# A transformer block on one core: three of four LN2 tiles and the attention probabilities transposed by VectorE and DMA instead of TensorE

## The chip, the core and the metric

The kernel runs on one NeuronCore of a Trainium2 chip. Five engines work side by side, each through its own instruction queue in order: TensorE (PE, matrix multiply; its weight loads are shown as PEld), VectorE (DVE), ScalarE (ACT), GpSimd (POOL) and SyncE (SP, which issues DMAs). They wait for each other by semaphores. The metric is the device time of one execution in microseconds (us), lower is better; the page and the traces time a profiled execution.

## What is computed

A diffusion-transformer block over 2 batches of 256 tokens, model width D = 1152, 2 heads of 576, feed-forward width F = 4608, all in bf16:

```
mod = (silu(c) @ w_mod).reshape(B, 6, 1, D)
shift_a, scale_a, gate_a, shift_m, scale_m, gate_m = [mod[:, i] for i in range(6)]
h = layernorm(x) * (1 + scale_a) + shift_a
q, k, v = (h @ wqkv) split by head
attn = softmax(q @ k.T * Dh ** -0.5)
x = x + gate_a * ((attn @ v) @ wo)
h2 = layernorm(x) * (1 + scale_m) + shift_m
return x + gate_m * (gelu(h2 @ w_fc1) @ w_fc2)
```

## The kernel before

The 512 tokens are four tiles of 128 (tiles 0 and 1 are batch 0, tiles 2 and 3 batch 1), the width D is KT = 9 chunks of 128, F is JT = 36 chunks. A matrix product needs its contracted dimension on the 128 partitions, so what LayerNorm and softmax leave with tokens on partitions has to be transposed before the next product.

The program records every operation with a cost (`S.op`, `S.unit`), finds the dependencies from the memory that operations read and write, and a list scheduler (`schedule`, line 281) fixes each engine's order. PE and SP keep the order in which the code records them. ACT, DVE and POOL are ordered by the planner: the ready operation with the longest remaining path goes first, by the planned costs. Waits on semaphores follow from the dependencies; two readers of one PSUM bank on different engines are ordered too. PSUM has 8 banks.

The steps around the change, in PE's order:

- q, k (the last 9 q and k chunks), then scores S for the four (batch, head) pairs, numbered `idx = 2*batch + head`, in the order idx 0, 2, 1, 3.
- `s_and_softmax` (line 993): DVE row maximum `smax` and `snb`; ACT `sexp` (two activations with row sums); DVE reciprocal `sri`; DVE `spn` multiplies the 128x512 probabilities by it (L1013).
- `pt_transposes` (line 1017): four PE transposes of 128x128 per idx into PSUM and one copy to SBUF, `PT_ev` (DVE or ACT). They stand between the products of `v_proj` (12 of 9 matmuls, 384 columns each, evacuated by ACT).
- `rows` (72 matmuls, shift and scale of the MLP), three more `v_proj`, then `pv_halves` and `pv`, which take the transposed probabilities `PTS` as moving operand.
- The attention gate: `attn_gate` (line 1056) sums 18 DVE operations `ga_b_kt` of 1.4 us, reduces them, and stores the gate row to DRAM from POOL's queue (`st_ga0`, `st_ga1`); SP loads it back broadcast to 128 partitions (`ld_g0`, `ld_g1`).
- `wo_tile(t)` (line 1153): three products of 384 columns; for each DVE `wo_t1` (L1165, times the gate, which frees the PSUM bank) and POOL `wo_x1` (L1166, plus x); then DVE `bn`, `aggr`, `veps`, POOL `rstd` (L744), DVE `nmr2` (L1170) and ACT `xn2` (L1171), which writes the normalized tile `XN2[t]`.
- `xn2_T(t)` (line 1175): nine PE transposes of that tile into two PSUM banks; nine operations `h2T` apply scale and shift on the way to `H2T`, on DVE (L1187) or ACT (L1190).
- `fc1_tile(f, tok0, ntok)` (line 1193): nine matmuls with `H2T` as moving operand, then ACT Gelu (L1200). The first F0 = 9 of 36 chunks are done for batch 0 alone (256 tokens), later for batch 1; the others for 512 tokens at once. `xn2_T(0)` stands before `wo_tile(3)`, `xn2_T(1)` before its last third, `xn2_T(2)` after four and `xn2_T(3)` after seven of the batch-0 fc1 chunks.
- `mlp_gate`: 18 long DVE operations after the last `h2T`; then fc2, 13 products of 36 matmuls.

SP's queue holds the weight loads in the recorded order; `ld_wo` follows the K projection, the fc1 quarters 0 and 1 follow `rows`, then the two gate loads, quarters 2 and 3, the MLP gate weights `ld_gm` and two parts of w_fc2.

Of the kernel before, what the change touches and what calls it, by code (L numbers as in the profile page):

```python
# [9 lines left out]
SEM_LAT = 120.0  # L10
# [161 lines left out]
class Sched:  # L172
    def __init__(self):
# [8 lines left out]
        self.first = {}  # L182

# [9 lines left out]
    def instr(self, fn, reads=(), writes=(), name="", unit=None, is_out=False):  # L193
# [10 lines left out]
        return ins  # L204

# [75 lines left out]
    def schedule(self, dma_bw=385.0, dma_issue=650.0, dma_lat0=900.0, dma_lat1=600.0, verbose=False):  # L281
# [44 lines left out]
        while scheduled < n:  # L326
# [39 lines left out]
            for f, uid in fin_now:  # L366
                for s in units[uid].succ:
                    ndeps[s.uid] -= 1
                    at = max(avail_time.get(s.uid, 0.0), f + (SEM_LAT if True else 0.0))
# [139 lines left out]
F0 = 9  # L509
# [34 lines left out]
def build_kernel(nc, x, c, wqkv, wo, w_mod, w_fc1, w_fc2, out):  # L544
# [5 lines left out]
    with (  # L550
# [62 lines left out]
        H2T = HK  # L613
        OT = sb(O_HX, 9216).rearrange("p (k t) -> p k t", k=KT)
        PP = [sb(O_P + i * 1024, 1024).rearrange("p (j k) -> p j k", j=2) for i in range(4)]
        PTS = [sb(O_PT + i * 1024, 1024).rearrange("p (j k) -> p j k", j=2) for i in range(4)]
# [351 lines left out]
        dma(WO, wo_v, D * D * 2, "ld_wo", run=2304)  # L968

# [23 lines left out]
        def s_and_softmax(b, h):  # L993
# [18 lines left out]
            rib = ri.unsqueeze(2).broadcast_to([P, 2, 256])  # L1012
            u = dve(c_dve_tt16(512), lambda e: e.tensor_tensor(out=pp, in0=pp, in1=rib, op=ALU.mult), [pp, ri], [pp], "spn_%d" % idx)  # L1013
            if idx % 2 == 1:
                S.order_after(ga_units[(1, 7) if idx == 1 else (0, 8)], u)

        def pt_transposes(b, h):
            idx = b * 2 + h
            bank = s_bank[(b, h)]
            S.unit("pe", 4 * c_mm(128), "PT_%d_%d" % (b, h))  # L1020
            for kjt in range(2):
                for jq in range(2):
                    tr(ps16(bank, kjt * 256 + jq * 128, 128), PP[idx][:, jq, kjt * 128:(kjt + 1) * 128], IDENT)
            copy_on("dve" if b == 0 else "act", PTS[idx].rearrange("p j k -> p (j k)"), ps16(bank, 0, 512), 512, True, "PT_ev%d" % idx)

        v_banks = [0, 1, 2]
        v_rr = [0]

        def v_proj(t, ci):
            bank = v_banks[v_rr[0] % 3]  # L1030
# [25 lines left out]
        def attn_gate():  # L1056
# [25 lines left out]
            last_red[0] = dve(200, lambda e: e.transpose(GTA, GBA), [GBA], [GTA], "ga_t")  # L1082
            lin = scratch[0].rearrange("b (g c) -> (b g) c", c=32)
            dma(lin[0:64].rearrange("(j p) c -> p j c", j=2), GTA[:, 0:64].rearrange("p (j c) -> p j c", j=2), 4096, "st_ga0", eng="pool")
            dma(lin[64:72], GTA[0:8, 64:96], 512, "st_ga1", eng="pool")
# [32 lines left out]
        PVB = [(6, 7, 0, 1), (3, 4, 0, 1)]  # L1118
# [229 lines left out]
```

## Time and profile before

| What | Value |
|---|---|
| Device time, 3 runs | 242.79 to 243.5 us, median 243.26 us |
| Span of the profiled execution, first to last instruction | 242.5 us |
| Median less that span | 0.76 us |
| Granted TensorE clock, mean | 0.993 |
| Scores to the end of `rows` and V, on PE | about 49 to 75.9 us |
| `pv` and `wo_tile`, on PE | 75.9 to 98.5 us |
| fc1, on PE | 98.5 to about 170 us; fc2 after it |
| HBM read | 50.15 MB, most of it before 155 us |

In the page, busy is the time in which an engine worked; each digit of the slices is a tenth of 6.06 us; idle time is put down to whoever ended it. In the timeline each row has start and duration in us, engine, source line, operation, tiles and count; a bracket gives the idle time before it. Starts of successive operations on one engine are closer than their durations, because neighbours overlap: a step below is the distance between starts.

### The profile page before, as it was taken

To read this page: it belongs to the slowest core of one execution; us is meant where nothing else is said; L and a number is where in the kernel's file an instruction comes from. 1 tells how busy PE (TensorE), PEld (TensorE's weight loads), DVE (VectorE), ACT (ScalarE), POOL (GpSimd) and SP (SyncE) were. 2 spreads that over 40 slices of the span, in tenths; PEclk is the share of its full clock that TensorE was granted. 3 is DMA by queue.
4 is the path that set the end of the run, shared out by engine and by line. 5 is a ranking of instruction groups with operands and counts; after the bars stand their busy time and mean duration, and the time that the engine had idled before them with its cause. 6 is when DMAs were issued, how large, how long until landed. Compare 5 with 4: busy or idle time off the path is not lost.

```text
span 242.5 us, 3957 instructions
## 1 busy us (share of the span) xinstructions
PE 237.3 (98%) x1699; PEld 145.4 (60%) x1699; DVE 121.5 (50%) x229; ACT 67.8 (28%) x136; POOL 19.9 (8%) x36
## 2 busy tenths in 40 slices
PE   6899999999999999999999999999999999999995
PEld 2688844466666666898544444444666566566564
DVE  2654379988996689669999700000022222111112
ACT  4921440435524206973233322222000000000000
POOL 1300000000002276400000110000000000000000
PEclk9979999999999999999999999999999999999999
DMA  6999999999992999999963499100000000000000
GB/s 221 378 370 392 389 392 390 398 413 402 391 352 79 312 374 391 391 348 398 352 198 83 157 313 374 43 0 3 0 16 19 16 16 16 19 16 16 21 27 20
DMA packets 30363, 51.58 MB, mean 213 GB/s; under 512 B 1547, under 2 KB 15755, under 8 KB 30347
## 3 DMA queue, kind: packets, MB, share of 16 engines
q1 hardware_dynamic: 29888, 50.73, 58.9%
q0 software_dynamic: 288, 0.60, 0.8%
q8 instruction: 13, 0.21, 0.4%
q10 hardware_dynamic: 171, 0.01, 0.0%
q14 instruction: 3, 0.02, 0.0%
HBM read 50.15 MB, written 1.19 MB: 212 GB/s over the span
## 4 chain that ended last, share of the span: by engine, by line
PE 95%; DMA 3%; SPq 1%; DVE 0%; issue 0%
PE psum L692 93%; DMA arena<-in_wqkv_dram 3%; PE psum L695 2%; SPq L673 1%; DVE arena L1290 0%; DVE arena L1291 0%
## 5 line engine op out<-in xcount | busy, mean ns | idle before, releaser
L692 PE MATMUL psum<-arena 128*128 128x384 bf16 (+8 forms) x1610 | 234.0, 314 | 2.4 <-POOL arena L718 1.5
L692 PEld LDWEIGHTS psum<-arena 128*128 128x128 bf16 (+2 forms) x1610 | 139.7, 97 | 92.4 <-issue 3.8
L1290 DVE TENSOR_TENSOR arena<-psum,arena 128x384 f32<-128x384 f32 (+2 forms) x13 | 6.8, 526 | 88.6 <-PE psum L692 88.6
L1200 ACT ACTIVATE arena<-psum 128x512 bf16<-128x512 f32 (+1 forms) x45 | 22.8, 512 | 42.1 <-PE psum L692 42.1
L687 ACT ACTIVATE arena<-psum 128x512 bf16<-128x512 f32 (+6 forms) x34 | 18.2, 560 | 37.9 <-PE psum L692 37.9
L1064 DVE SCALAR_TENSOR_TENSOR arena<-arena 128x1152 f32<-128x1152 bf16 x16 | 21.9, 1408 | 0.0
L1095 DVE SCALAR_TENSOR_TENSOR arena<-arena 128x1152 f32<-128x1152 bf16 x16 | 21.4, 1414 | 0.0
L1166 POOL TENSOR_TENSOR arena<-arena 128x384 f32<-128x384 f32 x12 | 10.9, 912 | 11.7 <-DVE arena L1165 9.5
L740 DVE BATCH_NORM_STATS2 arena<-arena 128x6 f32<-128x384 f32 (+1 forms) x18 | 9.5, 549 | 3.8 <-DMA arena<-in_x_dram 3.8
L673 POOL DMA_DIRECT2D dit_scratch<-arena x4 | 2.4, 609 | 96.6 <-DVE arena L1082 60.3
L689 DVE CAST arena<-psum 128x512 bf16<-128x512 f32 x11 | 7.2, 687 | 5.3 <-PE psum L692 5.3
L1165 DVE TENSOR_TENSOR arena<-psum,arena 128x384 f32<-128x384 f32 x12 | 6.7, 556 | 3.7 <-PE psum L692 3.7
L1171 ACT ACTIVATE arena<-arena 128x1152 bf16<-128x1152 f32 x4 | 5.4, 1344 | 9.8 <-DVE arena L1170 9.8
L695 PE MATMUL psum<-arena 128*128 128x128 bf16 (+1 forms) x89 | 7.4, 225 | 0.4 <-DMA arena<-in_c_dram 0.4
L695 PEld LDWEIGHTS psum<-arena 128*128 128x128 bf16 (+1 forms) x89 | 6.3, 102 | 2.2 <-DMA arena<-in_c_dram 1.1
L1291 DVE TENSOR_TENSOR arena<-arena 128x384 bf16<-128x384 f32 (+2 forms) x13 | 6.9, 527 | 0.5
L1190 ACT ACTIVATE arena<-psum,arena 128x128 bf16<-128x128 bf16 x16 | 6.1, 455 | 3.0 <-PE psum L695 2.2
L1187 DVE TENSOR_SCALAR arena<-psum,arena 128x128 bf16<-128x128 bf16 x20 | 5.5, 336 | 2.9 <-PE psum L695 2.9
L1009 ACT ACTIVATE arena<-psum,arena 128x256 bf16<-128x256 f32 x8 | 3.7, 471 | 0.2 <-DVE arena L1006 0.2
L744 POOL TENSOR_TENSOR arena<-arena 128x1 f32<-128x1 f32 x6 | 3.3, 555 | 4.7 <-DVE arena L743 4.5
L1005 DVE TENSOR_REDUCE arena<-psum 128x2 f32<-128x512 f32 x4 | 2.8, 688 | 0.9 <-PE psum L692 0.7
L962 ACT ACTIVATE arena<-arena 128x256 bf16<-128x256 bf16 x6 | 2.5, 495 | 1.5 <-DVE arena L956 1.5
(60 smaller groups left out, 53.9 us busy)
## 6 DMA issues: line engine op xcount, KB each, us to landing
arena<-in_w_fc_dram SPq DMA_DIRECT2D x9, 1152.0 KB, 8.0
arena<-in_w_fc_dram SPq DMA_DIRECT2D x4, 2592.0 KB, 17.6
arena<-in_wqkv_dram SPq DMA_DIRECT2D x18, 288.0 KB, 9.3
arena<-in_w_mod_dram SPq DMA_DIRECT2D x6, 864.0 KB, 12.3
arena<-in_w_mod_dram SPq DMA_DIRECT2D x3, 1728.0 KB, 20.5
arena<-in_wqkv_dram SPq DMA_DIRECT2D x1, 2592.0 KB, 17.6
arena<-in_wo_dram SPq DMA_DIRECT2D x1, 2592.0 KB, 24.9
arena<-in_w_mod_dram SPq DMA_DIRECT2D x1, 2592.0 KB, 18.5
```

What stands on the lines that cost most here:

```text
L687: act(c_act(n), lambda e: e.activation(out=dst, in_=src, func=ACTF.Copy), [src], [dst], name)
L689: return dve(c_dve_psum16(n) if psum16 else c_dve_psum32(n), lambda e: e.tensor_copy(dst, src), [src], [dst], name)
L692: S.instr(lambda e: e.matmul(o, lhsT=l, rhs=r, start=st, stop=sp, **kw), reads=[l, r], writes=[o])
L695: S.instr(lambda e: e.transpose(o, i_, idn), reads=[i_, idn], writes=[o])
L740: dve(550, lambda e, s=s, o=o: e.bn_stats(out=o, in_=s), [s], [o], "bn_%s_%d" % (tag, ci))
L1064: ga_units[(b, kt)] = dve(150 + FG * 1.1, lambda e, o=o, w=w, s1=s1: e.scalar_tensor_tensor(out=o, in0=w, scalar=s1, in1=o, op0=ALU.mult, ...
L1095: u = dve(1300, lambda e, o=o, w=w, s1=s1: e.scalar_tensor_tensor(out=o, in0=w, scalar=s1, in1=o, op0=ALU.mult, op1=ALU.add), [w, s1, o], ...
L1165: dve(550, lambda e, o=o, ga=ga, x1c=x1c: e.tensor_tensor(out=x1c, in0=o, in1=ga, op=ALU.mult), [o, ga], [x1c], "wo_t1_%d_%d" % (t, ci))
L1166: S.op("pool", 930, lambda e, xs=xs, x1c=x1c: e.tensor_tensor(out=x1c, in0=x1c, in1=xs, op=ALU.add), reads=[x1c, xs], writes=[x1c], name=" ...
L1200: act(c_act(ntok), lambda e: e.activation(out=dst, in_=o, func=ACTF.Gelu_apprx_tanh), [o], [dst], "gelu_%d_%d" % (f, tok0))
L1290: dve(c_dve_psum32(w), lambda e, o=o, gm=gm, t1=t1: e.tensor_tensor(out=t1, in0=o, in1=gm, op=ALU.mult), [o, gm], [t1], "fc2_t1_%d_%d" % ( ...
L1291: dve(c_dve_32(w), lambda e, t1=t1, x1c=x1c, ost=ost: e.tensor_tensor(out=ost, in0=t1, in1=x1c, op=ALU.add), [t1, x1c], [ost], "fc2_out_%d ...
```

## The change

The probabilities of all four idx and the LN2 tiles 0, 2 and 3 are transposed without PE. DVE's transpose turns 32x32 blocks, inside groups of 32 partitions; the source is read with a stride so that four DMAs, one per group of 32 tokens, put each turned group onto all 128 partitions with contiguous runs (256 B for the probabilities, 576 B for LN2). The result lies in groups of 32 tokens, and the fc1 and PV operands are read in that form. `spn` moves from one DVE operation per idx to two ACT operations. Scale and shift of the moved tiles work in place in SBUF. Tile 1 keeps its PE transposes.

```diff
+            for jq in range(2):
+                o, aa = pp[:, jq, :], ri[:, jq:jq + 1]
+                act(c_act(256, 1), lambda e, o=o, aa=aa: e.activation(out=o, in_=o, func=ACTF.Copy, scale=aa), [o, aa], [o], "spn_%d_%d" % (idx, jq))
+            src, flat = pp.rearrange("p j (t x c) -> p c (j t) x", t=2, c=4), PTF[idx]
+            dve(c_dve_32(512), lambda e: e.transpose(flat, src), [src], [flat], "PT_turn%d" % idx)
+            for a in range(4):
+                dma(PPF[idx][:, 128 * a:128 * a + 128], flat[32 * a:32 * a + 32, :], P * 256, "mv_pt%d_%d" % (idx, a), run=256)
...
+        H2T = sb(O_HK, 9216).rearrange("p (g k i) -> p k g i", g=16, k=KT)
...
+        TURNED = {0: H2F[3], 2: XN2[0], 3: XN2[1]}
+        def xn2_turn(t):
+            src, flat = XN2[t].rearrange("p (k x c) -> p c k x", k=KT, c=4), TURNED[t]
+            dve(c_dve_32(D), lambda e: e.transpose(flat, src), [src], [flat], "h2turn_%d" % t)
+        def xn2_move(t):
+            b, b0 = t // 2, 0
+            for a in range(4):
+                dma(H2F[t][:, 288 * a:288 * a + 288], TURNED[t][32 * a:32 * a + 32, :], P * 576, "mv_h2_%d_%d" % (t, a), run=576)
+            for kt in range(KT):
+                dst = H2T[:, kt, 4 * t:4 * t + 4, :]
...
+                if kt % 2 if t == 0 else kt % 3 == 2:
+                    act(330, lambda e, dst=dst, s1=s1, s2=s2: e.activation(out=dst, in_=dst, func=ACTF.Identity, scale=s1, bias=s2),
+                        [dst, s1, s2], [dst], "h2T_%d_%d" % (t, kt))
+                    continue
+                last_h2T[0] = dve(220, lambda e, dst=dst, s1=s1, s2=s2: e.tensor_scalar(out=dst, in0=dst, scalar1=s1, scalar2=s2, op0=ALU.mult, op1=ALU.add),
+                    [dst, s1, s2], [dst], "h2T_%d_%d" % (t, kt))
```

`st_ga0` and `st_ga1` go from POOL's queue to SP's. The recorded order after the scores becomes:

```diff
-        v_proj(0, 2)
-        pt_transposes(0, 0)
...
+        dma(WO, wo_v, D * D * 2, "ld_wo", run=2304)
         wfc1_load(0)
-        wfc1_load(1)
+        gate_store()
         for b in range(2):
             dma(GA[b], scratch[0, b].partition_broadcast(P), P * D * 2, "ld_g%d" % b, run=2304)
+        wfc1_load(1)
+        v_proj(0, 2)
+        for t in range(1, 4):
+            for ci in range(NCH):
+                v_proj(t, ci)
+        rows()
         wfc1_load(2)
         wfc1_load(3)
...
         wo_tile(0)
+        xn2_turn(0)
+        xn2_move(0)
+        dma(WGM, wmod_v[:, :, 5 * D:6 * D], D * D * 2, "ld_gm", run=2304)
         wo_tile(1)
         wo_tile(2)
-        xn2_T(0)
+        xn2_turn(2)
         wo_tile(3, {2: lambda: xn2_T(1)})
-        for f in range(0, 4):
-            fc1_tile(f, 0, 256)
-        xn2_T(2)
...
+        xn2_turn(3)
+        xn2_move(2)
+        xn2_move(3)
+        for tok0 in (0, 128):
+            for f in range(0, 3):
+                fc1_tile(f, tok0, 128)
+        for f in range(3, F0):
             fc1_tile(f, 0, 256)
+        wfc2_load(1)
+        wfc2_load(2)
```

F0 rises from 9 to 14: three fc1 chunks are done for tile 0 and for tile 1 apart (128 columns), eleven for batch 0. On ACT, DVE and POOL the order of the softmax, gate and LN2 operations is written out by hand (`in_order`) instead of left to the planner; in it, DVE does `h2T_0` and `h2T_1` between the LN2 statistics of tiles 2 and 3, and the planner puts three Gelus of 128 tokens ahead of ACT's four `h2T_1`:

```diff
+        S.in_order("dve", ["wo_t1_0_0", "wo_t1_0_1", "bn_ln2_0_0", "wo_t1_0_2", "bn_ln2_0_1", "wo_t1_1_0", "bn_ln2_0_2", "aggr_ln2_0", "veps_ln2_0", "wo_t1_1_1", "nmr2_0",
+                           "bn_ln2_1_0", "wo_t1_1_2", "bn_ln2_1_1", "h2turn_0", "wo_t1_2_0", "bn_ln2_1_2", "aggr_ln2_1", "veps_ln2_1", "wo_t1_2_1", "nmr2_1", "bn_ln2_2_0", "wo_t1_2_2", "bn_ln2_2_1", "wo_t1_3_0", "bn_ln2_2_2", "aggr_ln2_2", "veps_ln2_2", "h2T_0_0", "h2T_0_2", "wo_t1_3_1", "nmr2_2", "h2T_0_4", "h2T_0_6", "h2T_0_8",
+                           "h2T_1_0", "h2T_1_1", "h2T_1_2", "h2T_1_3", "h2T_1_4", "bn_ln2_3_0", "wo_t1_3_2", "bn_ln2_3_1", "h2turn_2", "bn_ln2_3_2", "aggr_ln2_3", "veps_ln2_3", "nmr2_3"])
+        S.in_order("act", ["xn2_0", "xn2_1", "h2T_0_1", "h2T_0_3", "h2T_0_5", "h2T_0_7", "h2T_1_5", "h2T_1_6", "h2T_1_7", "h2T_1_8", "xn2_2"])
```

More of the change, by code (lines that the diff above doesn't have):

```diff
@@ L204, in instr, with in_order @@
         return ins
+    def in_order(self, eng, names):
+        by_name = {u.name: u for u in self.units if u.eng == eng}
+        for a, b in zip(names, names[1:]):
+            if by_name[a] not in by_name[b].deps:
+                by_name[b].deps.add(by_name[a])
+                self.loose.add((by_name[a].uid, by_name[b].uid))
     def order_after(self, u, prev):
@@ L508 @@
 NCH = 3
-F0 = 9
+F0 = 14
 KC = 5
@@ L1011, in s_and_softmax @@
             dve(165, lambda e: e.reciprocal(out=ri, in_=rsum), [rsum], [ri], "sri_%d" % idx)
[L1012 to L1026, printed above, removed]
+            for jq in range(2):
[5 more added lines that the diff above has]
+                dma(PPF[idx][:, 128 * a:128 * a + 128], flat[32 * a:32 * a + 32, :], P * 256, "mv_pt%d_%d" % (idx, a), run=256)
+        v_banks = [7, 0, 1, 2]
         v_rr = [0]
         def v_proj(t, ci):
-            bank = v_banks[v_rr[0] % 3]
+            bank = v_banks[v_rr[0] % 4]
             v_rr[0] += 1
@@ L1137, in pv @@
                 for kjt in range(2):
-                    mm(ps32(bank, half * 256, 256), V[:, 2 * b + kjt, g * 128:(g + 1) * 128], PTS[idx][:, kjt, :], kjt == 0, kjt == 1)
+                    mm(ps32(bank, half * 256, 256), V[:, 2 * b + kjt, g * 128:(g + 1) * 128], PTS[idx][:, kjt], kjt == 0, kjt == 1)
             tok = slice(b * 256, (b + 1) * 256)
@@ L1299, in build_kernel @@
             sems = {e: es.enter_context(nc.semaphore("c_" + e)) for e in ENGINES}
-            dma_sems = [es.enter_context(nc.semaphore("d%d" % i)) for i in range(60)]
+            dma_sems = [es.enter_context(nc.semaphore("d%d" % i)) for i in range(66)]
             S.emit(nc, block, sems, dma_sems)
```

67 lines of the change are left out of this document (32 added, 35 removed).

## The prediction

> **What bounds the kernel now.** I read the slices and the busy line first, then the chain of waits, then the timeline of PE.
>
> ```profile
> span 242.5 us, 3957 instructions
> ...
> PE 237.3 (98%) x1699; PEld 145.4 (60%) x1699; DVE 121.5 (50%) x229; ACT 67.8 (28%) x136; POOL 19.9 (8%) x36
> ...
> PE   6899999999999999999999999999999999999995
> ...
> PE 95%; DMA 3%; SPq 1%; DVE 0%; issue 0%
> ```
>
> PE is full from the third slice on, 95% of the chain is PE's own work, and the work on it is the time. An edit gains what it takes off PE's queue, and loses what PE then has to wait for.
>
> The timeline of PE shows what a group of transposes is worth, by the start of what follows it:
>
> ```profile
> 60.98 0.39 PE L695 MATMUL psum<-arena 128*128 128x128 bf16 x4
> 61.21 3.09 PE L692 MATMUL psum<-arena 128*128 128x384 bf16 x18
> ...
> 93.09 0.67 PE L695 MATMUL psum<-arena 128*128 128x128 bf16 x9
> 93.59 3.09 PE L692 MATMUL psum<-arena 128*128 128x384 bf16 x18
> ```
>
> **What comes off PE, and what goes on.** Four groups of probabilities at 61.21 - 60.98 = 0.23 are 0.9 us; three LN2 tiles at 93.59 - 93.09 = 0.50 are 1.5 us; together 2.4. Against it, Gelus of 256 tokens follow each other by 0.983 us (111.47, 112.46, 113.44) and those of 512 by 1.943, so each of the five chunks that are now split costs 2 x 0.983 - 1.943 = 0.023, 0.12 in all. The six products of 128 columns have 54 matmuls; at the transposes' 0.50/9 = 55.6 ns (they too load 128x128 weights each) they take 3.0 us in place of three times 0.983: 0.05. Credit: 2.4 - 0.17 = 2.23 us.
>
> The Trainium skill speaks against those 54: "TensorE: Matmul & The Clock Gate", section "Back-to-back issue gap", gives about 81 ns for 128 columns in a stream where each matmul has its weight load. By it they would cost 54 x 25 = 1.4 us more; the trace's 55.6 ns disagrees.
>
> The operand in groups of 32 tokens: `rows` already streams 288 columns in groups of 32 with gaps. Its 72 matmuls, four side by side, fill the time between the V evacuations at 69.17 and 73.04 less one V product of 1.46: 2.41 us, 134 ns for 288 columns, 0.47 ns a column against 162.5/384 = 0.42 elsewhere, with 18 group changes in it. I take no loss.
>
> **Work moved beside PE, at nothing.** Probabilities: DVE loses four `spn` (0.69) and two `PT_ev` (0.42) and gets four turns of 512 elements; transposes of 288 and 1152 take 0.43 and 1.36, so some 0.67 each. DVE is 0.9 us better off. ACT gets eight of 0.42 (hx, 6 in 2.50) where it was half idle. The last turn ends about 64: the V product after S of idx 3 is followed by transposes at 59.30, so S ended 1.46 earlier, at 57.8; then come ACT's exponentials and, on DVE, three turns and three gate sums of 1.4 ahead of it. SP then issues 16 moves at 0.42 (gate loads, 0.82 for two); the last four leave by 65.7 and land by 70 even at the 4.3 us of the gate loads. PV needs them at 75.9 - 0.9 = 75.0: 5 us of cover.
>
> Queued behind these moves on SP: `ld_wo`, then at 65.7; 2592 KB at 390 GB/s are 6.8 us, landing by 75; needed at 79.0. The fc1 quarter behind it ends about 77, and the gate stores, which had POOL's queue to themselves, now queue behind both. The gate loads wait for them and start about 77.2 (now 77.02) and land at 81.5. The first `wo_t1` could start at 81.59 - 0.9 = 80.7, so it is 0.8 late; four PSUM banks hold 5.8 us of `wo`, and the second (82.1) is on time. Cost nothing; beyond 4 us later it would stop PE.
>
> **The LN2 chain, which is not covered.** Rows I step with:
>
> ```profile
> L1171 ACT ACTIVATE arena<-arena 128x1152 bf16<-128x1152 f32 x4 | 5.4, 1344 | 9.8 <-DVE arena L1170 9.8
> L1190 ACT ACTIVATE arena<-psum,arena 128x128 bf16<-128x128 bf16 x16 | 6.1, 455 | 3.0 <-PE psum L695 2.2 <-PE psum L692 0.8
> ...
> L1200 ACT ACTIVATE arena<-psum 128x256 bf16<-128x256 f32 x18 | 6.7, 383 | 5.6 <-PE psum L692 5.6
> ```
>
> `wo_t1` number i is due at 80.7 + 1.463i. Tile 0: `bn` ends 86.1, `rstd` 87.2, `xn2_0` 88.85, turn (1.3) 90.3, four moves issued by 92.1, landed 93.7 at the 1.6 us of the output stores (96 KB). ACT does its four `h2T_0` after `xn2_1` (to 94.0), DVE its five between other work by about 97.2. PE ends `wo` at 98.48 - 0.9 - 0.5 = 97.1: no wait. Tile 0's three products end at 98.6.
>
> Now the wait. On ACT the four `h2T_1` stand behind the three 128-token Gelus, and the third waits for PE's product at 98.6: 0.2 to notice, some 0.25 to run, then four `h2T_1` at their step 0.385 (three in 1.16): ready at 100.65. PE needs the last chunk at 99.1. It waits 1.6 us; behind it are all fc1 products. `wo_t1_3_2`, whose bank that product takes, is done about 99.6, so it is hidden in the same wait. A Gelu and shift of this shape are not in the trace: at the 0.17 of ACT's 128x18 operation the wait is 0.7, at the 0.495 of a 128x256 one 2.0; the shift is nearly L1190's, so I take 1.6.
>
> Tile 3 follows from the same point: `xn2_2` 1.4, turn 1.4, statistics 1.8, `xn2_3` behind a Gelu 1.6, turn 1.4, moves 1.3 to the last issue and 1.9 to land, shift 1.3: 12.1 us after 100.65. PE has 1.1 + 11 x 0.983 = 11.9 us before it asks, and asks chunk by chunk. I add 0.1.
>
> Bounds: a move of 72 KB inside SBUF between 1.4 (20 KB store) and 4.3 us (gate loads); nearest the stores, 1.6 to 1.9. A DVE shift in SBUF between 0.15 (one column) and 0.27 (from PSUM): 0.7 us over six. A turn of bf16 between 0.7 (half) and 2.7 (double the row), 1.3 us a turn either way and two of them in tile 3's chain; the small turns of 96 columns take 0.27 in bf16 and 0.28 in f32, so I take the f32 row's time.
>
> Sum: 242.5 - 2.23 + 1.6 + 0.1 = 242.0 us of span. The median of the runs shown is 0.76 above the span before; with that, **242.8 us**.
>
> **Rivals.**
>
> *The waits shrink, faster.* If ACT's short operations run nearer the lower bound, and tile 3 arrives in time, 0.7 us or nothing remains: 241.0 to 241.9; 242.5 is reached where the wait is 1.3. For it: the shapes are smaller than the rows I used, and PE ends where it is out of work to hide. Against: ACT's order ties `h2T_1` to PE's own progress.
>
> *DVE and POOL exclude each other, slower.* The profile shows it:
>
> ```profile
> 89.54 0.91 POOL L1166 TENSOR_TENSOR arena<-arena 128x384 f32<-128x384 f32 x1
> 89.84 0.62 DVE L1170 SCALAR_TENSOR_TENSOR arena<-arena 128x1 f32<-128x1 f32 x1
> ...
> 100.77 0.16 DVE L1170 SCALAR_TENSOR_TENSOR arena<-arena 128x1 f32<-128x1 f32 x1
> ```
>
> A 0.16 us operation on DVE took 0.62 and ended with POOL's (90.45). In the new order `nmr2_0`, `nmr2_1` become ready just as POOL can start the next `wo_x1`, and the in-place `h2T_0` on DVE meet `wo_x1_3_1` (due 96.7). Each collision holds DVE up to 0.9, and its hand-written order passes that on to `h2T_1` and `wo_t1_3_2`. Three cost some 2 us beyond mine: span 243.9, 244.6 us; it decides from two on. Against: the starts are within 0.1 us of a tie, and in-place shifts may not collide at all. The Trainium skill has the rule in "SBUF — State Buffer", section "Who interferes with whom": DVE in its two-port modes, or with two SBUF inputs, and GpSimd hold a shared port for a whole instruction each. The rows above agree.
>
> *Moves land late, slower.* At 4.3 us tile 3's chain is 2.4 longer, 2.1 of it on PE: 244.9 us. Against: the 1.6 us of the stores, and a queue that is empty then.
>
> *The grouped operand streams slower.* All of fc1 is 71 us of PE; at `rows`' 0.47 against 0.42 it would lose 8 us: 251. Against: four matmuls side by side explain those.
>
> **How the numbers follow.** A measurement here tells from no change about 0.3%, 0.73 us: 242.53 to 243.99. My forecast (own range 242.5 to 243.4) lies inside: 0.40. Faster, waits shrunk: 0.32. Collisions 0.15, late moves 0.09, slow operand 0.04: slower 0.28. The range goes down to 241.3, where a wait of 0.3 remains, and up to 244.8, past the three collisions and short of late moves at their worst.
>
> **What would show it.** PE's timeline: a gap before the products of tile 1 near 99 to 101 of about 1.6 us, ended by ACT's L1195, and little or none where fc1 turns to tokens 256 to 511; 128-column matmuls 56 ns apart; 256-column steps still 0.983. The moves' time to landing near 1.8. `nmr2` of 0.16 or 0.6 tells the collisions. I am wrong if PE waits in `pv` or `wo` (gate or WO late), if the gap is ended by a DMA, or if fc1 steps grow.

## The result and the profile after

| | Device time, median (range) | against before |
|---|---|---|
| before, run beside it | 243.18 us (242.79 to 243.5) | |
| after | 249.01 us (248.74 to 249.46) | 1.0243, 95% interval 1.0226 to 1.0261 |

The change makes the kernel 5.8 us slower. The prediction said 242.8 us, within 241.3 to 244.8: wrong by 6.2 us, and on the other side of before.

The page of the changed kernel, its span, busy time, PE's slices and the chain of waits:

```profile
span 247.1 us, 4079 instructions
...
PE 236.2 (96%) x1728; PEld 146.4 (59%) x1728; DVE 126.0 (51%) x231; ACT 71.2 (29%) x149; POOL 18.8 (8%) x34
...
PE   6999999999999896699998999999999999999996
...
PE 76%; DMA 12%; DVE 9%; POOL 1%; ACT 1%; issue 0%; ACTq 0%; DVEq 0%
```

PE has about 1 us less to do than before (236.2 against 237.3 busy), and its row now has holes in slices 14, 16, 17 and 22. PE's share of the chain fell from 95% to 76%; a DMA and VectorE took the rest. The timeline of PE shows the holes; the bracket is the idle time and who ended it:

```profile
84.51 10.67 PE L703 MATMUL psum<-arena 128*128 128x384 bf16 x63 [0.83 <-DVE arena L1170]
97.37 0.68 PE L706 MATMUL psum<-arena 128*128 128x128 bf16 x9 [2.19 <-ACT arena L1176]
97.88 1.93 PE L703 MATMUL psum<-arena 128*128 128x384 bf16 x13
101.03 1.68 PE L703 MATMUL psum<-arena 128*128 128x128 bf16 x23 [1.22 <-DVE arena L1215]
103.67 30.87 PE L703 MATMUL psum<-arena 128*128 128x128 bf16 x270 [0.95 <-DVE arena L1170]
135.34 109.30 PE L703 MATMUL psum<-arena 128*128 128x512 bf16 x648 [0.81 <-DMA arena<-in_w_fc_dram]
```

There are five waits: in `wo` (the gate product L1170 late), ahead of tile 1's transposes (its normalisation L1176 late), ahead of the first fc1 products (tile 0's in-place shift, L1215), ahead of the first product on tile 1 (an accumulation bank that L1170 has to empty), and at the seventeenth fc1 step (a weight quarter). They add up to 6.0 us by these rows, and to more by position. From the last PSUM evacuation of `pv` (80.13 before, 77.86 after) to the start of the last 648 matmuls (130.77 and 135.34, 109.30 us ahead of the end of the last matmul in both) the kernel took 50.64 us before and takes 57.48 now, 6.84 more. By the prediction's count it saves 1.33 us there (three tiles' transposes less the cost of the split products), so some 8.2 us were lost; less these 1.33, and less the 0.9 that it counts ahead of `pv`, 5.9 remain, about the time measured. The rows show less because the ends of matmuls are modelled and a matmul that is held up looks longer.

The wait at 103.67 is one such place. The bank comes free there, but the last of the nine chunks of tile 1 is ScalarE's:

```profile
102.93 1.50 ACT L1195 ACTIVATE arena<-psum,arena 128x128 bf16<-128x128 bf16 x4
```

These four shifts end at 104.43. TensorE starts eight matmuls from 103.67 to 104.13 and the ninth only at 104.48; the view of L1195 has one wait on it, 0.3 us, of a weight load. So the first product on tile 1 waits some 1.25 us in all, and ScalarE's shifts end it.

The two profiles' spans are not compared: the profiled execution of before had a granted clock of 0.68 from 12 to 16 us, which the one of after didn't, so spans start about 1 us apart. Medians carry the comparison.

SP's queue, first column start, second duration in us:

```profile
54.35 11.70 SPq L684 DMA_DIRECT2D arena<-arena  x16
66.09 0.59 SPq L684 DMA_DIRECT2D arena<-in_wo_dram  x1
66.72 0.60 SPq L684 DMA_DIRECT2D arena<-in_w_fc_dram  x1
73.13 0.75 SPq L684 DMA_DIRECT2D dit_scratch<-arena  x2
80.22 0.82 SPq L684 DMA_DIRECT2D arena<-dit_scratch  x2
```

The sixteen moves of the probabilities, WO and the fc1 quarter leave as forecast. The gate's stores leave at 73.13, as soon as the gate is there. But the loads that read them back can go only at 80.22: the view of DMA issues gives this 4 KB store 7.1 us to landing, where it took 1.8 before. VectorE's timeline has the consequence:

```profile
83.90 1.02 DVE L1170 TENSOR_TENSOR arena<-psum,arena 128x384 f32<-128x384 f32 x2 [5.34 <-DMA arena<-dit_scratch]
```

The first `wo_t1` is due 1.46 us after the last evacuation of `pv` (81.59 against 80.13 before), at 79.32. It came 4.6 us late.

Last, VectorE and POOL side by side, from the timeline of all engines:

```profile
89.27 0.98 DVE L1175 SCALAR_TENSOR_TENSOR arena<-arena 128x1 f32<-128x1 f32 x1 [0.19 <-POOL arena L755]
89.33 0.90 POOL L1171 TENSOR_TENSOR arena<-arena 128x384 f32<-128x384 f32 x1
...
95.01 0.91 POOL L1171 TENSOR_TENSOR arena<-arena 128x384 f32<-128x384 f32 x1
95.07 0.86 DVE L1175 SCALAR_TENSOR_TENSOR arena<-arena 128x1 f32<-128x1 f32 x1 [0.19 <-POOL arena L755]
...
99.85 0.15 DVE L1175 SCALAR_TENSOR_TENSOR arena<-arena 128x1 f32<-128x1 f32 x1
99.92 1.29 DVE L1215 TENSOR_SCALAR arena<-arena 128x128 bf16<-128x128 bf16 x2
100.01 0.91 POOL L1171 TENSOR_TENSOR arena<-arena 128x384 f32<-128x384 f32 x1 [0.48 <-DVE arena L1175]
```

`nmr2` (L1175), 0.15 us when alone, takes 0.98 and 0.86 beside a POOL add, and ends with it. Two in-place shifts take 1.29 us beside one; two alone took 0.54 a microsecond earlier. All three collisions that the prediction named took place. The `nmr2` at 99.85 met no add and took 0.15.

### The profile page after: what moved, and what is told of

Read it like the earlier page. It is cut to its first block, busy times and chain, and to the rows that moved or that the text cites. A ratio compares the mean times of both kernels' runs of the same rounds, so it can differ in the third digit from the quotient of the medians.

```text
span 247.1 us, 4079 instructions
## 1 busy us (share of the span) xinstructions
PE 236.2 (96%) x1728; PEld 146.4 (59%) x1728; DVE 126.0 (51%) x231; ACT 71.2 (29%) x149; POOL 18.8 (8%) x34
## 4 chain that ended last, share of the span: by engine, by line
PE 76%; DMA 12%; DVE 9%; POOL 1%; ACT 1%; issue 0%; ACTq 0%; DVEq 0%
PE psum L703 75%; DMA arena<-in_w_fc_dram 6%; DMA dit_scratch<-arena 3%; DVE arena L1067 3%; DMA arena<-in_c_dram 2%; DMA arena<-dit_scratch 1%; DVE arena L1073 1%; DVE arena L1075 1%; PE psum L706 1%; DVE arena L1170 1%; DVE arena L1025 1%; POOL arena L1171 1%; DVE arena L1215 1%; ACT arena L1195 1%; DVE arena L751 0%
## 5 line engine op out<-in xcount | busy, mean ns | idle before, releaser
L703 PE MATMUL psum<-arena 128*128 128x384 bf16 (+9 forms) x1682 | 234.0, 307 | 5.9 <-DVE arena L1170 1.8
L703 PEld LDWEIGHTS psum<-arena 128*128 128x128 bf16 (+2 forms) x1682 | 143.9, 97 | 93.9 <-issue 4.3
L1225 ACT ACTIVATE arena<-psum 128x256 bf16<-128x256 f32 (+2 forms) x53 | 24.1, 460 | 44.2 <-PE psum L703 44.1
L698 ACT ACTIVATE arena<-psum 128x512 bf16<-128x512 f32 (+5 forms) x33 | 17.7, 558 | 32.1 <-PE psum L703 32.1
L1176 ACT ACTIVATE arena<-arena 128x1152 bf16<-128x1152 f32 x4 | 5.4, 1349 | 16.2 <-DVE arena L1175 16.2
L1170 DVE TENSOR_TENSOR arena<-psum,arena 128x384 f32<-128x384 f32 x12 | 6.4, 540 | 5.3 <-DMA arena<-dit_scratch 5.3
L1215 DVE TENSOR_SCALAR arena<-arena 128x128 bf16<-128x128 bf16 x17 | 4.9, 350 | 3.0 <-DMA arena<-arena 3.0
L706 PE MATMUL psum<-arena 128*128 128x128 bf16 (+1 forms) x46 | 3.5, 219 | 2.6 <-ACT arena L1176 2.2
L1202 DVE STREAM_TRANSPOSE arena<-arena 128x1152 bf16<-128x1152 bf16 x3 | 4.1, 1379 | 3.2 <-ACT arena L1176 3.2
L706 PEld LDWEIGHTS psum<-arena 128*128 128x128 bf16 (+1 forms) x46 | 2.8, 98 | 4.1 <-ACT arena L1176 2.6
L1212 ACT ACTIVATE arena<-arena 128x128 bf16<-128x128 bf16 x10 | 4.3, 484 | 0.6 <-DMA arena<-arena 0.6
L1023 ACT ACTIVATE arena<-arena 128x256 bf16<-128x256 bf16 x8 | 3.6, 502 | 0.2 <-DVE arena L1020 0.2
## 6 DMA issues: line engine op xcount, KB each, us to landing
arena<-in_w_mod_dram SPq DMA_DIRECT2D x6, 864.0 KB, 13.3
```

The costliest lines, as they stand in the source:

```text
L698: act(c_act(n), lambda e: e.activation(out=dst, in_=src, func=ACTF.Copy), [src], [dst], name)
L703: S.instr(lambda e: e.matmul(o, lhsT=l, rhs=r, start=st, stop=sp, **kw), reads=[l, r], writes=[o])
L706: S.instr(lambda e: e.transpose(o, i_, idn), reads=[i_, idn], writes=[o])
L1170: dve(550, lambda e, o=o, ga=ga, x1c=x1c: e.tensor_tensor(out=x1c, in0=o, in1=ga, op=ALU.mult), [o, ga], [x1c], "wo_t1_%d_%d" % (t, ci))
L1215: last_h2T[0] = dve(220, lambda e, dst=dst, s1=s1, s2=s2: e.tensor_scalar(out=dst, in0=dst, scalar1=s1, scalar2=s2, op0=ALU.mult, op1=ALU. ...
L1225: act(c_act(ntok), lambda e: e.activation(out=dst, in_=o, func=ACTF.Gelu_apprx_tanh), [o], [dst], "gelu_%d_%d" % (f, tok0))
```

## The experiments

Two theories at the start. A: the gate, late behind the weight loads, is the loss. B: the LN2 order itself is, with VectorE and POOL holding each other up. All medians below stand beside medians of before of 242.93 to 243.05, and each ratio is against before.

### The gate's stores back on POOL's queue (e1_gate_pool)

```diff
-            dma(lin[0:64].rearrange("(j p) c -> p j c", j=2), GTA[:, 0:64].rearrange("p (j c) -> p j c", j=2), 4096, "st_ga0")
-            dma(lin[64:72], GTA[0:8, 64:96], 512, "st_ga1")
+            dma(lin[0:64].rearrange("(j p) c -> p j c", j=2), GTA[:, 0:64].rearrange("p (j c) -> p j c", j=2), 4096, "st_ga0", eng="pool")
+            dma(lin[64:72], GTA[0:8, 64:96], 512, "st_ga1", eng="pool")
```

> The changed kernel with the two gate stores back on POOL's queue; the gate loads stay on SP behind WO and the first fc1 quarter. Theory A (the gate waits behind the weight loads in SP's queue): stores land about 2 us after issue instead of 7, but the loads' own data still stands behind the fc1 quarter, which ends near 79.7, so the gate lands about 82.5 instead of 83.9: 247.2 to 247.8 us. Theory B (the LN2 order itself, with DVE and POOL holding each other up, is what costs): no change, 248.5 to 249.3 us.

Measured 248.71 us, 1.0224 (1.0181 to 1.0266): no gain, as theory B forecast. But the store did not land sooner either, as the view of DMA issues shows:

```profile
dit_scratch<-arena POOLq DMA_DIRECT2D x1, 4.0 KB, 5.8
```

On POOL's queue the store still took 5.8 us and landed at 80.0, where it landed at 80.2 in the change. So it is not the queue that it stood in: by the windows of this kernel WO and the fc1 quarter, 3.7 MB, had the DMA engines to over 1.0 of their share from 70 to 78 us and to 0.94 until 79, at 350 to 410 GB/s up to 78, and the store landed 1 us after that. The gate loads left at 80.02. Theory A named the right place, as the next run shows, and the wrong mechanism.

### WO loaded at its old place (e2_wo_early)

```diff
         proj(WK, 8, 17, HK, 7)
+        dma(WO, wo_v, D * D * 2, "ld_wo", run=2304)
...
         s_and_softmax(1, 1)
-        dma(WO, wo_v, D * D * 2, "ld_wo", run=2304)
```

> The changed kernel with ld_wo back at its old place, ahead of the probabilities' moves; gate stores still on SP, now behind the first fc1 quarter alone, which is issued near 66.7 and gone by 71. Theory A: stores land near 75, the gate near 79.3, when the first wo product is due; 244.0 us (243.2 to 245.0). Theory B: 247 us or more, since the LN2 order is the same. The probabilities' moves then queue behind WO until about 67, which is harmless before PV at 73.6.

Measured 246.58 us, 1.0142 (1.0102 to 1.0183): 2.4 us less than the change (2.2 when each is taken against its own before), between the two forecasts. The store took 4.6 us and the first `wo_t1` came at 81.97. TensorE's wait for it in `wo` is gone, and the wait ahead of tile 1's transposes fell from 2.19 to 1.05 us. The three collisions stayed: 0.97 and 0.87 us for `nmr2`, and 1.50 us for the three shifts that took 1.51 in the change.

### One half of the change at a time (e3_pt_only, e4_ln2_only)

The first turns only the probabilities, with WO and the gate queued as in the change; the second turns only LN2's tiles, with F0 = 14 and the hand-written orders of `wo` and LN2, and leaves probabilities, gate and WO as before.

> Only the first half of the change: probabilities turned and moved, WO and gate queued as in the changed kernel; LN2, fc1 and their loads as before. Theory A: the gate still lands about 5 us after its product, PE waits for PSUM banks and later for tile 0 and 1: 245 to 247 us. Theory B: the late gate is caught up, 0.9 us of transposes saved: 242.3 to 243 us.

Measured 244.66 us, 1.0076 (1.0050 to 1.0101). TensorE waits 0.97 us in `wo`, for L1170, and 1.10 ahead of tile 0's transposes.

> Only the second half: LN2 tiles 0, 2, 3 turned and moved with the hand-written LN2 orders and F0 = 14; probabilities by PE transposes, WO early and gate stores on POOL as before. Theory A: gate on time, 243 us (242.3 to 244.2), PE waits about 1.6 us once near 99. Theory B: three collisions of DVE and POOL and their sequel remain, 245 us or more.

Measured 247.89 us, 1.0182 (1.0133 to 1.0232). Both halves lose, 1.7 and 5.0 us (against 242.94). Two of the four executions of the LN2 half had a mean granted clock of 0.993 and took 248.5 us; the other two had 1.00 and took 247.0 and 247.3, a loss of 4.2. With that figure the halves add up to 5.9, what the whole change loses; with the median they come to 0.9 more. The LN2 half has the gate on time (first `wo_t1` 80.57) and still all three collisions.

### The collisions taken away, in two steps (e11_nmr_only, e5_no_collide)

On the LN2 half alone. First `nmr2` is divided, so that VectorE's part runs ahead of `rstd` and the product is POOL's own; then the in-place shifts of tile 0 also move ahead of `wo_t1_3_1`, whose result POOL's add waits for.

```diff
-            dve(170, lambda e: e.scalar_tensor_tensor(out=nm, in0=m, scalar=-1.0, in1=rs, op0=ALU.mult, op1=ALU.mult), [m, rs], [nm], "nmr2_%d" % t)
+            dve(140, lambda e: e.tensor_scalar(out=m, in0=m, scalar1=-1.0, scalar2=None, op0=ALU.mult), [m], [m], "nm_%d" % t)
+            S.op("pool", 650, lambda e: e.tensor_tensor(out=nm, in0=m, in1=rs, op=ALU.mult), reads=[m, rs], writes=[nm], name="nmr2_%d" % t)
...
-"h2T_0_0", "h2T_0_2", "wo_t1_3_1", "h2T_0_4", "h2T_0_6", "h2T_0_8",
+"h2T_0_0", "h2T_0_2", "h2T_0_4", "h2T_0_6", "h2T_0_8", "wo_t1_3_1",
```

> LN2's half alone (247.89) with nmr2 alone divided between VectorE and POOL; the in-place h2T_0 stay on both sides of wo_t1_3_1, beside a wo_x1 add. Both repairs together took 244.9. If each collision costs its own stall: nmr2's two take 1.6 to 2 us away and h2T_0's keeps 0.9: 245.7 to 246.3. If nmr2 alone set the loss, since the later stall lies beside another wait: 244.7 to 245.2. If h2T_0's alone did: 247 or more.

Measured 245.80 us, 1.0102 (1.0070 to 1.0134): 2.1 us less than the LN2 half's median. That is more than the two stalls themselves (0.99 and 0.86 us for 0.15 each, 1.5 in all). In the trace of the LN2 half the granted clock also fell after the waits (last section), and here it is 1.00 in all four executions; against the LN2 half's two executions at 1.00 the step is 1.35 us, about the stalls.

> The LN2 half alone (that kernel took 247.89 us, +4.95 against before), with the mixed operation nmr2 of each tile divided between VectorE (a negation right behind veps) and POOL (the product with rstd), and all five in-place VectorE h2T_0 put ahead of the evacuation wo_t1_3_1. Theory B1 (what stretches the order is VectorE and POOL holding each other up): no VectorE operation on sixteen-bit tiles or on 128x1 columns runs beside a wo_x1 add any more; VectorE's chain up to tile 1's normalisation loses two stalls of 0.8 and one of 0.9 us; the waits of 1.23 and 0.95 us of TensorE before the first fc1 steps shrink to under 0.6 together; time 245.3 to 246.5. Theory B2 (the order itself, with the in-place and PSUM evacuations of tile 1 behind the Gelus on ScalarE, the lost weight-load cover and the clock that falls after the waits, costs the most): the stalls go, but the same waits stay to within 0.3 us; time 247.4 to 248.3.

Measured 244.90 us, 1.0076 (1.0062 to 1.0090): 0.9 less again, 3.0 in all. VectorE's `nm` takes 0.14 us and five in-place shifts 1.22. The wait ahead of the first fc1 products, 1.23 us in the LN2 half, is gone; with `nmr2` alone divided some 0.4 of it was left (the 36 matmuls from tile 1's transposes to the next wait take 3.54 us there, 3.13 here). So the three collisions cost 3.0 us by the medians in this half, and 2.25 at a granted clock of 1.00.

### Probabilities alone, WO early, with the store on either queue (e12_pt_wo_early, e6_pt_gate_pool)

The probabilities' half with WO at its old place, the gate's stores on SP and on POOL's queue.

> Probabilities turned, WO loaded at its old place, the gate's stores still on SP behind the sixteen moves and fc1's first quarter (with them on POOL as well it took 242.34; with WO late and the stores on SP 244.66). If 2.6 MB of WO ahead of the gate is what costs: gate loads land about 82, first wo_t1 some 2.5 us late, four accumulation banks take most of it: 242.4 to 243.1. If the queue of moves and the fc1 quarter ahead of the stores is enough: TensorE waits about 1 us in the output projection, 243.3 to 244.2.

Measured 242.23 us, 0.9972 (0.9950 to 0.9993).

> Probabilities turned and moved as in the change, LN2 and fc1 as before, but WO loaded at its old place and the gate's two stores on POOL's queue (the kernel with the same parts and the changed queue order took 244.66). Theory A (a gate queued behind 3.7 MB of weights is what makes this half a loss): the gate loads land by 78, the first wo_t1 runs within 0.3 us of its accumulation's end, TensorE waits under 0.3 us in the output projection; the saved transposes (0.9 us of TensorE) then show: 242.0 to 242.6, ratio 0.996 to 0.999. Rival A2 (the softmax and move chain itself is late, or the moves delay the projections' weights): TensorE waits 0.5 us or more ahead of PV, or the gate is late still; 243.0 to 245.

Measured 242.34 us, 0.9976 (0.9966 to 0.9985). The two agree, and TensorE has no wait in `wo` in either: the store's queue makes no difference that shows, WO's place makes 2.4 us (244.66 to 242.23). In the first the store took 4.0 us, and the first `wo_t1` came 1.5 us late, which TensorE's four accumulation banks hide. This half gains 0.7 us once WO is early; the prediction's 0.9 us of transposes was nearly right.

### Tiles 2 and 3 alone (e7_ln23, e8_pt_ln23)

Kernel before, tiles 2 and 3 turned and moved, tiles 0 and 1 on TensorE, the planner's own order, F0 = 9; the second has the mended probabilities' half too.

```diff
-        for f in range(0, 4):
-            fc1_tile(f, 0, 256)
-        xn2_T(2)
-        for f in range(4, F0 - 2):
-            fc1_tile(f, 0, 256)
-        xn2_T(3)
-        for f in range(F0 - 2, F0):
+        for t in (2, 3):
+            xn2_turn(t)
+            xn2_move(t)
+        for q4 in range(1, 3):
+            dma(WFC2[:, 9 * q4:9 * q4 + 9, :], wfc2_v[:, 9 * q4:9 * q4 + 9, :], 9 * P * D * 2, "ld_wfc2_%d" % q4, run=2304)
+        for f in range(F0):
             fc1_tile(f, 0, 256)
```

> The kernel before with LN2 tiles 2 and 3 alone turned by VectorE and moved; tiles 0 and 1 on TensorE, no order written by hand, nothing else moved but the two second-weight quarters behind the moves on SP. Theory B (the loss of the LN2 half sits in tile 0's move, the hand order and the early 128-token steps): two tiles' transposes (2 x 0.50 us) leave TensorE, tile 3 is ready some 4 us before fc1 needs tokens 256 to 511, no new wait: 242.0 to 242.5, ratio 0.996 to 0.998. Rival (turning and moving is itself a loss here: the moves land late, the grouped operand is slower, or the later second-weight loads stop TensorE): a wait of TensorE over 0.5 us at the first step of the second token half or at an fc1 weight quarter; 243.0 to 245.

> The last two together: probabilities turned with the gate on POOL's queue, LN2 tiles 2 and 3 turned, tiles 0 and 1 on TensorE in the planner's order. If both theories hold the credits add: 0.9 + 1.0 us, 241.0 to 241.6, ratio 0.992 to 0.995, faster than both kernels. If only one half gains: 242.0 to 242.5. If the later weight loads collide with the moves: a wait of TensorE ended by a DMA from the fc1 weights of 0.5 us or more, 242.5 to 244.

Measured 250.43 us, 1.0313 (1.0293 to 1.0333), and 249.12 us, 1.0265 (1.0244 to 1.0287). All forecasts missed by far: these kernels are slower than the change (e7) or as slow (e8), for one wait. The windows of the first, two microseconds each (busy time of PE, its weight loads, VectorE, ScalarE and POOL, then the granted clock, DMA share and GB/s):

```profile
104.00:106.00 2.00, 2.00 (x20) 1.80 (x19) 0.82 (x1) 0.97 (x4) 0.00 (x0) 1.00 0.27 65
106.00:108.00 2.00, 0.83 (x8) 0.49 (x6) 0.02 (x1) 0.70 (x3) 0.00 (x0) 1.00 0.45 114
108.00:110.00 2.00, 0.00 (x0) 0.00 (x0) 1.41 (x6) 1.22 (x3) 0.00 (x0) 0.98 0.45 111
110.00:112.00 2.00, 0.98 (x5) 0.60 (x6) 1.35 (x7) 1.26 (x3) 0.00 (x0) 0.50 0.80 188
112.00:114.00 2.00, 2.00 (x12) 1.38 (x11) 2.00 (x4) 0.38 (x1) 0.00 (x0) 0.50 1.03 402
114.00:116.00 2.00, 2.00 (x11) 1.44 (x10) 2.00 (x2) 0.38 (x1) 0.00 (x0) 0.50 1.05 408
```

Nine early steps of 0.98 us were over at 106.8, and tile 3's last shift ended at 112. TensorE stood for 4.2 us, and then ran at a granted clock of 0.50 for six more: the window from 112 to 114 has 12 matmuls of 256 columns, where a window at full clock has 20 or 21. Half of six microseconds is 3 us more: a stop of 4.2 us cost some 7.2, an estimate from these windows. In the second kernel the stop is 4.03 us, and the windows from 110 to 114 are at 0.50 too.

### Both repairs on the whole change (e9_both_mended)

WO early, the stores on POOL, `nmr2` divided, the shifts ahead of `wo_t1_3_1`.

> The whole change with both repairs: WO loaded at its old place and the gate's stores on POOL's queue (probabilities' half), nmr2 divided between VectorE and POOL and the five in-place h2T_0 ahead of wo_t1_3_1 (LN2's half). If the two losses are separate and these two are all that the change lost beyond what is left of LN2's order, the parts add: 242.99 - 0.65 (probabilities with the gate mended) + 1.9 (LN2's half without the collisions) = 244.2, 243.8 to 244.7. If the halves hinder each other besides (PT's moves or its evacuations on ScalarE against LN2's start): 245 or more.

Measured 245.09 us, 1.0071 (1.0050 to 1.0092). The two repairs give back 3.7 of the 5.8 us. What the probabilities' half gains does not show. TensorE is ahead by some 1.1 us at the start of `wo` (the first `wo_t1` would be due at 79.9, where the mended LN2 half, e5, had it at 81.00), but the gate's store takes 4.5 us and `wo_t1` starts at 82.15. Tile 0's normalisation then starts at 87.81, against 87.89 in e5, and the first product on tile 1 at 99.75, against 99.85: the chain through VectorE, SP and ScalarE sets these times, and 2 us of a late gate that the planner's order hides are not hidden here. ScalarE's part of that chain, from its timeline:

```profile
95.74 1.65 ACT L1214 ACTIVATE arena<-arena 128x128 bf16<-128x128 bf16 x4 [1.41 <-DMA arena<-arena]
97.41 1.28 ACT L1227 ACT_TABLE_LOAD   x1
98.70 0.61 ACT L1227 ACTIVATE arena<-psum 128x128 bf16<-128x128 f32 x3
99.19 1.52 ACT L1197 ACTIVATE arena<-psum,arena 128x128 bf16<-128x128 bf16 x4
```

It waits for tile 0's moves, then works without a break: tile 0's shifts, a table load of 1.28 us ahead of the first Gelu, three Gelus, and tile 1's shifts to 100.71. TensorE's matmuls on the last two chunks of tile 1 start at 100.41 and 100.76, behind these shifts. Here the table load is in the path of tile 0; in the kernel before it runs from 99.09 to 100.37 and TensorE has no wait beside it. No run moved it.

### The last two waits (e13_mended_wfc2, e14_mended_bank)

Both repairs, with one second-weight quarter ahead of the moves; then also the last `wo` evacuation ahead of tile 1's shifts.

```diff
+        wfc2_load(1)
         xn2_turn(3)
         xn2_move(2)
         xn2_move(3)
...
-        wfc2_load(1)
         wfc2_load(2)
```

```diff
-"wo_t1_3_1", "h2T_1_0",
+"wo_t1_3_1", "wo_t1_3_2", "h2T_1_0",
...
-"bn_ln2_3_0", "wo_t1_3_2", "bn_ln2_3_1",
+"bn_ln2_3_0", "bn_ln2_3_1",
```

> The whole change with both repairs (245.09) and, besides, the first of the two second-weight quarters put ahead of the moves of tiles 2 and 3 on SP, behind the MLP gate's weights; the other stays behind them, ahead of fc1's fifth quarter. There TensorE waited 0.94 us for that quarter at its seventeenth fc1 step. If the order of these loads is that wait: the quarter lands before 131, the wait goes, 244.0 to 244.4. If the moves are then held up by the load ahead of them: they land 2 us later, still 5 us before TensorE wants tile 2, and nothing is lost. If the wait only moves elsewhere: 245 again.

Measured 245.06 us, 1.0070 (1.0049 to 1.0092): the wait moved. The moves of tiles 2 and 3 stood behind the load and took 5.3 us to land (2.2 otherwise), and now TensorE waits for their shifts, by its timeline:

```profile
113.69 0.51 PE L703 MATMUL psum<-arena 128*128 128x256 bf16 x2 [0.89 <-DVE arena L1217]
114.47 125.70 PE L703 MATMUL psum<-arena 128*128 128x256 bf16 x758 [0.27 <-ACT arena L1214]
```

> As the last one, and the output projection's last evacuation (wo_t1_3_2) put ahead of the five h2T_1 on VectorE; it ended the 1.02 us wait of TensorE ahead of the fourth fc1 step, whose accumulation bank it holds, and not the PSUM evacuations of tile 1 that the step also reads. If the bank is what stops TensorE: the wait goes to under 0.5 us and 0.5 us or more are gained on the last one. If tile 1's evacuations on ScalarE (behind the Gelus, done at 100.7) come last anyway: the same wait, ended by ScalarE, and the same time within 0.3.

Measured 245.22 us, 1.0075 (1.0053 to 1.0098): nothing gained. That agrees with tile 1's shifts on ScalarE coming last anyway, as in e9 and e13, where the last chunk's matmul starts at 100.76. The profiled execution of e14 took 872.31 us, where the other eight took 244.3 to 245.84, so its own waits are not known.

### Sixteen early steps, and the version that beats both (e10_pt_ln23_f16)

The mended probabilities' half and tiles 2 and 3 turned, as in e8_pt_ln23, with F0 = 16 and one second-weight quarter ahead of the moves.

```diff
-F0 = 9
+F0 = 16
...
+        wfc2_load(1)
         for t in (2, 3):
             xn2_turn(t)
             xn2_move(t)
-        for q4 in range(1, 3):
-            dma(WFC2[:, 9 * q4:9 * q4 + 9, :], wfc2_v[:, 9 * q4:9 * q4 + 9, :], 9 * P * D * 2, "ld_wfc2_%d" % q4, run=2304)
+        wfc2_load(2)
...
+                if f == 24:
+                    wfc2_load(3)
                 wfc1_load(f // 4)
```

> Probabilities turned with the gate mended, LN2 tiles 2 and 3 turned and moved, tiles 0 and 1 on TensorE; sixteen in place of nine fc1 steps run on tokens 0 to 255 first, and one second-weight quarter stands ahead of the moves on SP instead of both behind. With nine steps tile 3 came at 112 where TensorE wanted it at 105.6: a wait of 4.0 us, then about 6 us at a granted clock of 0.50; that kernel took 249.12. If its loss was this wait and the clock after it: with sixteen steps TensorE wants tile 3 at about 112.5, no wait over 0.3 us, clock 1.00, and the transposes saved show: 241.0 to 241.8. If the turned tiles are a loss for another reason (late weights, the grouped operand): 242.5 or more.

Measured 241.58 us, 0.9930 (0.9903 to 0.9958): faster than both kernels. The moves landed in 4.0 us and tile 3's shifts ended at 111.9. TensorE comes to these tokens at about 111.9 too (`wo` over at 94.66 + 1.46, sixteen steps of 0.983), with no slack to spare. `nmr2` of tiles 0 and 1 still meets POOL's add here (0.87 and 0.85 us), and TensorE has no wait for it. Its timeline has one row from tile 1's transposes almost to the end, with no wait:

```profile
94.66 142.21 PE L703 MATMUL psum<-arena 128*128 128x384 bf16 x945
```

### Tile 0 turned as well (e15_tile0_too)

```diff
-        TURNED = {2: XN2[0], 3: XN2[1]}
+        TURNED = {0: H2F[3], 2: XN2[0], 3: XN2[1]}
...
         wo_tile(0)
+        xn2_turn(0)
+        xn2_move(0)
+        dma(WGM, wmod_v[:, :, 5 * D:6 * D], D * D * 2, "ld_gm", run=2304)
         wo_tile(1)
         wo_tile(2)
-        xn2_T(0)
```

> The last but two faster kernel's version with tiles 2 and 3 turned (241.58) and tile 0 turned and moved as well, in the planner's own order, fc1 still in steps of 256 tokens, the MLP gate's weights behind tile 0's move on SP. If tile 0's move is where LN2's half loses (turn, move and in-place passes stand between the normalisation and the first fc1 step, where nothing is left to run): TensorE waits 1 us or more ahead of the first fc1 steps, 242.5 to 244.5. If the loss was in the order written by hand and the steps of 128 tokens: a third 0.50 us of transposes is saved, 241.0 to 241.5.

Measured 244.29 us, 1.0050 (1.0038 to 1.0062): 2.7 us more than without. The timeline, all engines:

```profile
88.91 1.35 ACT L1177 ACTIVATE arena<-arena 128x1152 bf16<-128x1152 f32 x1 [10.32 <-DVE arena L1176]
90.29 1.38 DVE L1203 STREAM_TRANSPOSE arena<-arena 128x1152 bf16<-128x1152 bf16 x1 [0.21 <-ACT arena L1177]
...
94.67 0.68 PE L706 MATMUL psum<-arena 128*128 128x128 bf16 x9 [0.63 <-ACT arena L1177]
...
96.48 1.19 DVE L1216 TENSOR_SCALAR arena<-arena 128x128 bf16<-128x128 bf16 x5
...
97.11 1.65 ACT L1213 ACTIVATE arena<-arena 128x128 bf16<-128x128 bf16 x4
...
97.68 16.27 PE L703 MATMUL psum<-arena 128*128 128x256 bf16 x143 [0.56 <-ACT arena L1213]
```

Tile 0 is normalised at 90.26 and shifted to the end at 98.76, 8.5 us later; TensorE had its transposes started 0.6 us after the normalisation in the version without (90.08, 90.65). The turn stands in VectorE's queue ahead of tile 1's statistics, so tile 1's normalisation is late (0.63 us), and the shifts are late for fc1 (0.56 us). A third wait, 0.81 us at tile 2, ends with its shift: the moves of tiles 2 and 3 leave at 104.27 and take 6.1 us to land, where they left at 102.23 and took 4.0 without. The MLP gate's weights, which this edit puts behind tile 0's move, may have a part in that; no run parts the two.

## Why the prediction was wrong

- **The credit was right.** The mended probabilities' half gains 0.7 us (0.9 said), and with tiles 2 and 3 the kernel gains 1.4 us (0.9 + 1.0 less seven split steps at 0.023 would be 1.7). The grouped operand streams as fast as the plain one: steps of 256 columns follow each other by 0.98 us, and the Gelus of 128 tokens by 0.50, 55.6 ns a matmul. The rival of a slow operand is out.
- **First failed step: the gate behind WO on SP, "Cost nothing; beyond 4 us later it would stop PE".** The moves and the loads left as forecast, and WO landed at 75.7 (66.09 and 9.6; "by 75" said). The store was put at about 77 because WO and the fc1 quarter would be through by then; the quarter landed at 80.0 (66.72 and 13.3), the store at 80.2, the loads left 3.0 us later than the 77.2 said, and the first `wo_t1` was 4.6 us late instead of 0.8. This cost 2.2 to 2.4 us in the change (249.01 to 246.58) and 2.4 in the half alone. The working let the store land with the weights ahead of it; the engines were busy with these until 78 (windows), and the store came 2 us after. The bound of 4 us was written down, and crossed. The Trainium skill, in "DMA: Bandwidth & Descriptors", section "Issuing engines are not separate DMA queues", says that DMAs of all issuing engines run on the same 16 engines. The runs agree: beside the same loads the store took 7.1 us on SP's queue and 5.8 on POOL's, and 1.8 in the kernel before.
- **Second failed step: the collisions as a rival at 0.15.** All three happened. They cost 3.0 us in the LN2 half by the medians and 2.25 at a granted clock of 1.00, so the 2 us that the prediction put on them was near; what failed was to leave them out of the sum. The prediction had the row that shows them and the places where they would fall, "within 0.1 us of a tie". But for tiles 0 and 1 the end of POOL's `rstd` lets both `nmr2` and POOL's next add start, as the add's input is ready by then; the two start together by construction, not by chance. For tiles 2 and 3 no add stood ready, and `nmr2` took 0.15 and 0.16. The Trainium skill, in "SBUF — State Buffer", section "Who interferes with whom", says that a VectorE instruction with two SBUF inputs contends with a GpSimd instruction that reads SBUF. The trace agrees: 0.15 alone, 0.98 beside POOL.
- **Third failed step: tile 0, "PE ends `wo` at 98.48 - 0.9 - 0.5 = 97.1: no wait".** The path over the move was counted operation by operation and came out just in time, with no margin for a late `wo_t1` or a held VectorE. In the change TensorE waits 1.22 us there. With the planner's order, and the MLP gate's weights behind the move, it costs 2.7 us (e15 against e10), for one turn ahead of tile 1's statistics, 8.5 us from normalisation to the last shift, and later moves for tiles 2 and 3. Its own 0.50 us of transposes are never earned.
- **The 1.6 us wait on ScalarE** came where it was forecast: 0.95 us until the bank was free, and 0.3 more for the last of ScalarE's shifts (L1195, to 104.43). The place and the releaser were right, and the size was 1.25; taking the bank away changed nothing (e14).
- **The late-moves rival** did not happen for tile 3 in the change: the moves of tiles 2 and 3 took 2.2 us. Those of tile 0 took 3.1, where 1.6 was taken. In e13, where a load stood ahead of the moves of tiles 2 and 3, they took 5.3.
- **Not foreseen:** the seventeenth fc1 step's wait for its weight quarter, 0.81 us, as the moves hold back both second-weight quarters, and these the quarter. It can be traded for another wait on SP's order (e13), and is gone where the moves are fewer and sixteen steps cover them (e10). The table load of 1.28 us on ScalarE is not in the prediction's path either. In the change it costs nothing (99.30 to 100.58, and the first Gelu has its input at 101.75); with both repairs it is in the path (e9).

The sum of the runs, each against its own before: 5.8 us lost, 2.2 by the gate (3.6 left in e2) and some 1.5 by the collisions once the gate is mended (2.1 left in e9). Where the gate was never late the collisions cost 2.25 to 3.0, so part of the two losses seems to be shared. The 2.1 us that remain were not split to the end: tile 0's move (2.7 us in e15) is probably the main part, with ScalarE's unbroken work behind it, and what the 128-token steps and the hand-written order add or save beside it stays open.

## What to carry to other kernels

Work taken from a full engine pays only if the new path is ready when that engine asks: turn the tiles that are needed last (here tiles 2 and 3, with early steps enough to cover them) and leave on TensorE the tile whose consumer has nothing else to run. Before a large load is moved, list the small transfers in flight beside it, whatever their queue; here 2.6 MB of weights moved ahead of a 4 KB store on the critical path cost 2.4 us. Where the end of one POOL operation lets both a VectorE operation and a waiting POOL operation start, expect a collision like that of tiles 0 and 1, and ask whether the path behind it has slack: in e10 it had, and the collisions cost no wait.

## What the runs showed of the hardware

- After a stop of 4.2 us TensorE's granted clock was 0.50 for about 6 us (e7, above). In e4, after waits of 1.23 and 0.95 us within 4 us, it was 0.83, 0.50 and 0.81 in the three windows of 2 us from 100 on; the change itself, with waits of 2.19, 1.22 and 0.95 us, kept 1.00 there. That the waits lower the clock in e4 is not shown.
- VectorE's block transposes of bf16 took 1.38 us for 1152 elements and 0.71 for 512; for 1152 that is the time of f32 (1.36 us).
- Moves inside SBUF of 72 KB landed in 2.2 us on idle DMA engines, and in 4.0 to 6.1 behind a load of 2592 KB (e10, e13, e15).
- A VectorE operation on 128x1 columns, 0.15 us, took up to 0.98 us beside POOL, while shifts that read PSUM took 1.34 us for five both beside a POOL add (e5, from 97.53, the add from 97.68 to 98.59) and with none (the change, from 101.34).
